# A re-ordered opening, a re-drawn plan and a gate on MLP stages in a fused attention and MLP kernel

## The chip, the cores and the metric

The kernel runs on one core of a Trainium2 chip. The metric is the device time of one execution in microseconds. A core has five engines that the text names as the profile does: PE (matrix products; PEld is its loading of weights), DVE (vector), ACT (scalar functions), POOL and SP (here only the issuer of DMAs). Each engine runs its instructions in the order in which they were put on it and waits on semaphores for the others. All arithmetic is in float32.

## The reference

x has 2048 tokens of width 512. There are 32 query heads of width 16 with one shared key head and one value head; the MLP has 1792 hidden features.

```python
xn = layernorm(x)                       # no scale, no bias, eps 1e-5
q = heads(xn @ wq); k = xn @ wk; v = xn @ wv
p = softmax(q @ k.T * 16 ** -0.5)
a = merge(p @ v) @ wo
h = xn @ w1 + b1
act = h * tanh(softplus(h))             # Mish
return x + a + act @ w2
```

## The kernel before

**Precision.** Products with weights are made of three matmuls in a fast float32 form: operand and weight are each split into a high part (a copy on ACT) and a low part (a subtraction on POOL), and hi x hi, hi x lo and lo x hi are summed (TERMS). The function split (L165) does it for a block of weights: one ACT and one POOL instruction of 128x512 each. A block goes through a buffer raw (three of them, L186), and its split form is stored to DRAM for later use (kept).

**Tiles.** Tokens are handled in four chunks c of 512 (CT), each four tiles of 128. xn is held transposed as X[c]. The queries of four heads (a unit u, 32 units in all) come out of half a block of 128 columns of wq: queries(c, mt) makes two units with 12 products, one for each of 4 parts of the width and 3 terms. hidden(c, f) (L597) makes one MLP tile of 128 features x 512 tokens, also with 12 products; there are 56. outputs(c, part, t) multiplies three (the last group two) of the finished tiles with w2, finals(c, t) the attention with wo.

**Softmax.** For each unit the scores are computed twice: once in the layout query x key, of which DVE takes the row maxima (maxima, L382; first_maxima, L388 for unit 0), and once in the layout key x query with the maximum subtracted inside the product (exps, L437), of which ACT takes the exponential. To subtract the maximum, negate_maxima and place_maxima (L393, L401) reduce the maxima of a unit, transpose them on PE (mt), split them on DVE (mhl) and send them by four DMAs to rows 48 to 49 and 112 to 113 of the unit's query tile QS (send, L410). values (L462) multiplies the exponentials pt with V and a column of ones, eight PE records per step of 128 keys.

**MLP stages.** A hidden tile h (buffer th, three of them) goes through these stages: ACT adds the bias (th); exponential: ACT, u = exp(h) (tu); square: DVE clamps u; product: POOL, n = u (u + 2); quotient: ACT, z = ln(n + 2) and r = exp(-z), then POOL five instructions with a result in h; act: ACT and POOL split h into the tile act. Each stage is put in a list (later, L139) with the step and the modelled time from which it may be put on its engines. run_due takes what is due, and flush(tags) puts stages on their engines at once when something needs them.

**The opening** (L861 to L979) loads x, normalises it, transposes it, projects keys and values and makes all queries. At the same time a loop over 32 pairs of score tiles (order, L936) finds the maxima of unit 0. In it first_maxima takes a pair of PSUM banks (tag e, two such pairs in the pool first_ps), and between the pairs PE is given either a part of transposes(2), transposes(3), keys_values(2), keys_values(3) (beside, L927) or products of the pieces of fill (fill_slot, L845). A piece is a set of 12 products that can be asked for one at a time. The pieces asked for first are those in urgent, the 15 left of the queries (L866); hidden tiles and the rest come after them. The opening ends when all queries are made; then six products of the first hidden tile are done and the second half of unit 0's maxima is placed.

**The planned part** (L984 to L1064) is written out as a string, PLAN, of 4270 letters. A letter is either one group of values (".") or one lane step: PE's array is used as two halves of 64 rows (lanes 0 and 1), and a lane step gives each half one matmul. A half may get a score tile for a maximum, a score tile for an exponential (single: a bank of its own, wide: one of a pair), half a product of a piece of fill (half), or nothing. A letter with the mark d drains PE first. The string comes from a planner that is not part of the kernel; the class Clock (L1067) follows it with prices for each step and tells when the stages in the list are due, by a time t of its own. POOL's modelled time (free) stands in Counted.

**Banks.** PSUM has eight banks. Before: the pool ps, which lives throughout, holds m (2 banks), misc (1) and o (1); first_ps has two pairs (4); late_ps, which takes their place, has e2 (2), e1 (1) and one more m (1). mbank (L128) takes a bank of kind m in turn.

Of the kernel before, what the change touches and what calls it, by code (L numbers as in the profile page):

```python
# [9 lines left out]
F32 = mybir.dt.float32  # L10
# [47 lines left out]
    "QQtisiisROQQcsiisRQckkkGyQQUQOQyG.oCssMisiysq.oqo.GQyQOEQ.qwo.sMoCsisMisysMs.mwe.qQOQSSQOOQOG.QSoq.sCCssMsii"  # L58
    "ysMs.mAo.GQyQ.QQUQSSQOUQ.GoCsiMsisCCq.ssCRQSOQOQOOQOQ..GyQQOOUQOQyOUQQ.qmCCiiMsisysM.oqo.Gsiy.qssiiysM.wAss."
    "sCCsVQQQSSUQ.yQQQU.ysMssiisCCq.my.Gwo.UQQOyQUOQO.qsCCsiMsisy.Gmy.QASQQOQUOQ.ssAw.GQSSQOQUOQyQUQ.qwo.sMssCCsM"  # L60
    "is.qym.GQy.USSQQQU.GCCssiMsisy.qoS.sMsysisM.mGy.ssyRQUOQOQSUo.ssMCsCisiG..GSSQQOQOUQy.sMCCssG.qSSQQOUQOQyq.m"
    "CsC.mGy.QUSSQQQU.wqCsiisMisysMs.mCo.qwSQOU.sCCssMsiisCCq.myq.QQUQSSQOUQOQ.MsCCssMs.qwo.GwSQ.AQSQQOUQOOoSG.wC"
    "ssM.mwS.QUQQOOQOAo.GsCCsisiisG.SSQUQQOOQy.qys.sMCCsssM.qSSQQOUQOQy.qosC.sMssCCsq.QSQUSQQOOG.GCCssiq.ACsss.Gy"
    "QQOOUQOQSSUQ.mCMCs.qCsCsMsis.QUQSSQQUOQ.Awm.UyQ.qmCCiisiMsisyMs..GSwQOOUQOQSSUQ.yqm.ysMssiisCCMss.AwQQ.QUQQO"
    "SSq.ossMC.qmy.MsyssM.qQQSSOQOQU.GCCssiMsisy.qSSQQ.GSSQQOG.tssMCCsis.USSQQQU.GCCssiMsisy.qwQS.GQQy.GSSQQOUQQS"
    "SG.oCqs.sMCssCsMis.qwSQ.wSQQUOQOyQUQ.qwo.sMssCCsiiMss.Gym.AQSQQOUQOOSQS..oMsCsisMisCsMw.UQQQOSSUQ.omC.MCsssC"
    "iiq.QQUSSQQOU.GCCssisMisy.qmy.GQSSQUQ.GwoiiiMssy.UQQwS.QQqy.GsCCsMs.qwSQOOQUOQ.SQGSQ.qwoiiiMsisCCMss..GSSQQO"
    "UQQSSG.SQGw.qsys.qsCCsiMsisCw.UQQSSQUQ.wQAQ.ooq.sCCsMssiisCCq.moUS.sMssCCq.mAo.QGSSQQU.CsMCssRUQSQS.sMssCCs."
    "GsCRUSQQ.QSUSm.ssMsCCsMsPSQUSQQOQ..AsCssiMsiiysMs.Awm.GQSSQOUQOQOSS..qCCssiMsisy.Gmy.GSSQQOUQQSSG.wSQG.mMy.s"
    "sqy.ssMsCCsMRQSSQUQ.mSQA.ysG.yQQQUOOQSSG.oCqs.sMssCCs.qow.sMCCsssM.oMoRQUOQOyQUQ.wwQ.QUQSSQQU.GsCCsiMsis.QUQ"  # L70
    "SSQQ.GyQQOOU.qCCssiMsisCCq.ms.AwQOQOUQOSSQUQ..qmCCiiMsisysiMs.SwUQQOOQSSQUQ..qwoiiiMsisCCsis.QQAw.QQUSSQQjsi"
    "MsiyssM..yQUQQOOQOOykq.oMCssisMisy.qssy.qym.sMssCCsPUQQ.ASQQQU.ysMssiisCCG.owG.QQUSSQQOU..qyssiiMsisCCq.Csqo"
# [20 lines left out]
    "QQ.ASQm.GCCssMs.sMsysis.UQSwQOUQOOQSS..ACsssiMisiCsMw.UQSSQQ.USQQQSE.ysMssiisCCMss..UQSSQQUQOOQSNssCs.sMsCCs"
    "s.ASQQQU.QQUSSQQG.GCCssiq.Aom.MCCsssM.qSSQQOUQOQyOUQ..qwoiiiMsisCCMss.qwo.GSSQQOUQOQy.qwo.sMsCsCsiiG..wSQQUO"
    "OQSQUSQ.GwoiiiMsisCCMss..qQSSQOUQOQew.mMsCCisMis.QQUSSQQOU.yqssiiisCCs.Gym.qCCssiMsisy.qww.UQQQSSUQO..qCCssi"
    "Msisyq.yQG.yQQQUOOQy.Uy.siiMiiCCMPOOSSUO.AS.Uy.MiiiyiMiii.PUSSOOOEOO.MCCiig.ACiiig.ASOOOOUOOOy.MiCCiM.Vy.UOy"
    "OOU.CCM.yiMiPSSU.yOU.y.MCCiiMPSSU.yOU.y.MiyiiiMPyOU.yOOO.."
# [4 lines left out]
def attention_and_mlp(ctx: ExitStack, tc: tile.TileContext, x, wq, wk, wv, wo, w1, b1, w2, out):  # L102
# [34 lines left out]
    now, queue = [-100], []  # L137
# [115 lines left out]
    def transposes(c):  # L253
        xt, FLAT[c] = x_tile(c, first if c > 1 else work)
        n = 2 if c < 2 else 1
        for d in range(0, DT, n):
            pt = first_ps.tile([P, 2, CT], F32, tag="e", name=f"xt{c}_{d}", bufs=2) if c < 2 else mbank(f"xt{c}_{d}")[:, None]
# [64 lines left out]
    def queries(c, mt):  # L322
# [5 lines left out]
        turn[1] += 1  # L328
        p = bank("o", f"q{c}_{mt}", 1) if beside == [] and turn[1] % 2 else misc(f"q{c}_{mt}")
# [58 lines left out]
    def first_maxima(kc, qt, pair):  # L388
        e = first_ps.tile([P, 2, CT], F32, tag="e", name=f"s0_{qt}_{kc}_{pair}", bufs=2)
        m = score_tiles(0, qt, kc, pair, {0: e[:, 0], 1: e[:, 1]})  # L390
        DVE.tensor_reduce(out=m, in_=e, axis=AX.X, op=ALU.max)
# [9 lines left out]
    def place_maxima(u, pairs=slice(0, 2)):  # L401
# [8 lines left out]
        def send():  # L410
            for a in range(2):
                for part in range(2):
                    SP.dma_start(
                        out=QS[u][a * 64 + 48 + part : a * 64 + 49 + part, pairs].bitcast(F32),
                        in_=m[a * n // 2 : (a + 1) * n // 2, part].bitcast(F32),
                    )
# [172 lines left out]
    read = {"u": 0.0, "z": 0.0}  # L589
# [7 lines left out]
    def hidden(c, f):  # L597
# [15 lines left out]
        def exponential():  # L613
            flush(("u", k - 1), ("n", k - 2))
# [15 lines left out]
        def product(u, n):  # L630
# [3 lines left out]
            later(2, lambda: quotient(n), ("n", k), max(POOL.free, read["z"]))  # L634

        def quotient(n):
            if late_pool:
# [10 lines left out]
            read["z"] = POOL.free  # L648
# [8 lines left out]
        later(max(1, 8 + k - 100 - now[0]), exponential, ("u", k), read["u"])  # L657
# [202 lines left out]
    with tc.tile_pool(name="first", bufs=1) as first, tc.tile_pool(name="first_ps", bufs=1, space=PSUM) as first_ps:  # L860
# [5 lines left out]
        urgent += [queries(*divmod(i, DT)) for i in range(1, NC * DT)]  # L866
# [31 lines left out]
        load_tokens(3)  # L898
        ask()
        flush(("wq", 0))  # L900
# [9 lines left out]
        flush(("wq", 1))  # L910
# [27 lines left out]
        skip = True  # L938
        for i, (kc, qt, pair) in enumerate(order):
# [289 lines left out]
```

## Time and profile before

| what | value |
|---|---|
| median of three runs | 1763.2 us (1760.71 to 1764.64) |
| profiled execution, its own time | 1763.43 us |
| its span, first to last instruction | 1761.7 us |
| mean granted PE clock | 0.97 |
| busy PE, DVE, ACT, POOL | 95%, 78%, 76%, 45% of the span |
| first lane matmul of the planned part | 121.87 us |
| first matmul of the first group of values | 140.4 us |

In the profile, a row of the timeline gives start and length in us, the engine, the line of the kernel, the operation, the tile written and the tile read, the shapes, and how many instructions were merged (x). What stands in brackets is the idle time of the engine ahead of the row and the instruction that ended it. A line of the waits names the waiting engine, tile and line, then the one waited for, the total in us, the number of waits and the longest. PE's clock is the share of full speed that was granted to it. Lines 1176, 1180, 1192 and 1200 are those of a helper that records every DVE, POOL or ACT operation, so there the tile's name tells what it is.

### The profile page before, as it was taken

How to read it: one execution, taken by the hardware profiler on the slowest of the kernel's cores; microseconds unless marked ns; L12 is line 12 of the kernel's file. 1: busy time of each engine (PE TensorE's matmuls, PEld its weight loads, DVE VectorE, ACT ScalarE, POOL GpSimd, SP SyncE). 2: the span in 40 equal slices, each digit the busy share in tenths (PEclk: the TensorE clock that was granted, in tenths of full speed). 3: DMA queues.
4: the chain of work that ended last, by engine and by line, in shares of the span. 5: the costliest groups of instructions: out<-in, count | busy, mean ns of one | idle time of the engine just before them, and what ended most of it. 6: DMA issues, size and time to landing. Idle time of an engine off the chain costs nothing.

```text
span 1761.7 us, 29992 instructions
## 1 busy us (share of the span) xinstructions
PE 1668.1 (95%) x11567; PEld 879.9 (50%) x11567; DVE 1369.5 (78%) x2269; ACT 1334.4 (76%) x1992; POOL 787.6 (45%) x699
## 2 busy tenths in 40 slices
PE   5989789799999999999999999999999999999998
PEld 4564444455455445554554555555455544545544
DVE  6638658688888878788888888888888888888821
ACT  3327568688788878788688888788688888877885
POOL 4534445455735444545136355445226264441532
PEclk8988889899999999999999999999999999999999
DMA  5555100304222212123122222122221222122030
GB/s 175 201 197 197 52 19 29 123 28 147 99 77 85 99 40 64 52 80 137 47 90 73 85 70 76 52 76 64 70 97 61 84 76 76 52 94 82 19 132 25
DMA packets 66821, 149.90 MB, mean 85 GB/s; under 512 B 9430, under 2 KB 19734, under 8 KB 66422
## 3 DMA queue, kind: packets, MB, share of 16 engines
q1 hardware_dynamic: 66678, 147.98, 24.8%
q8 instruction: 91, 1.49, 0.4%
q14 instruction: 52, 0.43, 0.1%
HBM read 97.98 MB, written 49.02 MB: 83 GB/s over the span
## 4 chain that ended last, share of the span: by engine, by line
PE 76%; POOL 5%; ACT 5%; DVE 4%; issue 2%; DMA 1%; POOLq 0%; ACTq 0%; DVEq 0%
PE o L466 25%; PE e L449 14%; PE s L373 13%; PE y L799 10%; PE h L799 10%; DVE nm L1192 3%; ACT pt L1200 3%; PE f L799 2%; POOL th L1176 2%; POOL tn L1176 1%; POOL tz L1176 1%; ACT tr L1200 1%; PE f_last L564 1%; ACT tz L1200 1%; DMA raw_w<-in_B_w_dram 1%
## 5 line engine op out<-in xcount | busy, mean ns | idle before, releaser
L1192 DVE TENSOR_REDUCE nm<-s 128x1 f32<-128x512 f32 (+1 forms) x2016 | 1281.4, 691 | 291.8 <-PE s L373 194.9
L1200 ACT ACTIVATE pt<-e 128x1024 f32<-128x1024 f32 (+1 forms) x1430 | 1047.9, 781 | 248.8 <-PE e L449 167.8
L373 PE MATMUL s<-KS,QS 48*128 48x512 f32 x2048 | 748.4, 437 | 2.6 <-DVE nm L1192 1.5
L449 PE MATMUL e<-QS,KS 64*128 64x512 f32 x2048 | 692.6, 434 | 37.9 <-ACT pt L1200 37.1
L466 PE MATMUL o<-pt,V 128*32 128x512 f32 x4096 | 544.9, 610 | 0.0
L373 PEld LDWEIGHTS s<-KS,QS 48*128 48x128 f32 x2048 | 356.5, 189 | 218.1 <-DVE nm L1192 172.9
L449 PEld LDWEIGHTS e<-QS,KS 64*128 64x128 f32 x2048 | 327.6, 188 | 255.1 <-ACT pt L1200 193.1
L799 PE MATMUL y<-w,act 64*128 64x512 f32 x1344 | 375.2, 407 | 8.2 <-ACT ty L1200 4.8
L799 PE MATMUL h<-X,w 64*128 64x512 f32 (+1 forms) x1338 | 370.7, 410 | 11.4 <-ACT th L1200 6.2
L799 PEld LDWEIGHTS y<-w,act 64*128 64x128 f32 x1344 | 241.3, 188 | 79.8 <-issue 33.9
L799 PEld LDWEIGHTS h<-X,w 64*128 64x128 f32 (+1 forms) x1338 | 246.6, 191 | 68.8 <-issue 19.0
L466 PEld LDWEIGHTS o<-pt,V 128*32 128x32 f32 x4096 | 84.8, 108 | 172.9 <-issue 167.7
L1180 POOL TENSOR_SCALAR tn<-tu 128x512 f32<-128x512 f32 x56 | 34.8, 621 | 295.8 <-DVE tu L1188 295.8
L1176 POOL TENSOR_TENSOR tn<-tn,tr 128x512 f32<-128x512 f32 x56 | 72.2, 1290 | 193.3 <-ACT tr L1200 193.2
L1176 POOL TENSOR_TENSOR y<-y,ty 128x512 f32<-128x512 f32 x80 | 103.2, 1290 | 120.7 <-ACT ty L1200 120.7
L1176 POOL TENSOR_TENSOR act<-th,act 128x512 fp32r<-128x512 f32 x56 | 72.5, 1295 | 65.0 <-ACT act L1200 65.0
L799 PE MATMUL f<-wo,ohl 64*128 64x512 f32 x288 | 75.9, 400 | 2.9 <-DVE yf L1176 2.5
L1176 POOL TENSOR_TENSOR tz<-tz,tn 128x512 f32<-128x512 f32 x56 | 72.3, 1291 | 4.7
L1176 POOL TENSOR_TENSOR th<-th,tn 128x512 f32<-128x512 f32 x56 | 74.3, 1326 | 0.0
L1176 POOL TENSOR_TENSOR th<-th,tz 128x512 f32<-128x512 f32 x56 | 72.2, 1289 | 4.4
L1176 POOL TENSOR_TENSOR tn<-tn,tu 128x512 f32<-128x512 f32 x56 | 71.9, 1284 | 4.7
L1176 POOL TENSOR_TENSOR ohl<-oc,ohl 128x512 fp32r<-128x512 f32 (+1 forms) x16 | 20.6, 1287 | 108.9 <-ACT ohl L1200 108.9
(86 smaller groups left out, 879.1 us busy)
## 6 DMA issues: line engine op xcount, KB each, us to landing
w<-w_dram SPq DMA_DIRECT2D x84, 512.0 KB
w_dram<-w SPq DMA_DIRECT2D x28, 512.0 KB
QS<-q_dram SPq DMA_DIRECT2D x62, 192.0 KB
q_dram<-q SPq DMA_DIRECT2D x16, 512.0 KB
wo<-wo_dram SPq DMA_DIRECT2D x16, 512.0 KB
o_dram<-ov SPq DMA_DIRECT2D x31, 256.0 KB
raw_w<-in_B_w_dram SPq DMA_DIRECT2D x28, 256.0 KB
xs<-in_A_x_dram SPq DMA_DIRECT2D x16, 256.0 KB
```

What stands on the lines that cost most here:

```text
L373: PE.matmul(tile, QS[u][rows, pair, qt * P : (qt + 1) * P], KS[rows, kc * CT : (kc + 1) * CT], start=True, stop=True,)
L449: PE.matmul(bank, KS[rows, kt * P : (kt + 1) * P], QS[u][rows, pair], start=True, stop=True)
L466: PE.matmul(O[u][h * 32 : (h + 1) * 32], V[:, kt], PT[(u * KT + kt) * HG + h], start=kt == 0, stop=kt == KT - 1,)
L564: PE.matmul(LAST[t], OHL[NC - 1, mt][:, i, t * P : (t + 1) * P], RINGED[NC - 1, "wo", mt][:, j], start=mt == 0 and k == 0, stop=mt == DT - ...
L799: PE.matmul(self.p, w[rows], x[rows], start=self.first, stop=last)
L1176: return self.engine.tensor_tensor(out=out, **kw)
L1180: return self.engine.tensor_scalar(out, *args, **kw)
L1192: return self.engine.tensor_reduce(out=out, in_=in_, **kw)
L1200: return self.engine.activation(out, in_, func, **kw)
```

## The change

- **Banks.** The banks m leave the pool that lives throughout. first_ps has three pairs of banks instead of two; late_ps gets all three m. In the opening mbank takes the first bank of such a pair, and all transposes take a pair too (one bank of it is used for chunks 2 and 3).
- **Order of fill.** urgent is filled later. The first two pieces asked for are hidden(0, 0) and hidden(0, 1). The blocks wq 1 to 3 are asked for behind them. The blocks w1 0 and w1 1 are split where wq 0 and wq 1 were, and wq 1 directly ahead of the loop.
- **The loop.** After each second pair of scores, six products are asked for, or two parts of beside with two products and one product behind them. Blocks are split in each pass. The order of beside is transposes(2), keys_values(2), transposes(3), keys_values(3). The opening goes on until all queries and the two hidden tiles are done (24 products of hidden tiles instead of 6).
- **Sends.** The four sends of unit 0's maxima, made for each of its two halves, are issued on ACT instead of SP.
- **Gate.** exponential and quotient ask, when they are run and not forced by a flush, whether the modelled time has reached the end of POOL's work on the tile before and whether that tile's stage is still in the list. If so they put themselves back in the list. The time that they had been given when they were listed falls away.
- **Plan.** PLAN has 4223 letters: 512 groups of values as before, 3711 lane steps (3758 before), of which 46 drain first (37 before). Halves of products: 2928 (2964 before); halves left empty: 462 (520 before). Clock.placed of unit 0 is 6.0 instead of 10.0.

```diff
 PLAN = (
...
-    turn, beside = [0, 0], [None]
+    turn, beside = [0], [None]
+
+    def pair_bank(name):
+        return first_ps.tile([P, 2, CT], F32, tag="e", name=name, bufs=3)
 
     def mbank(name):
-        turn[0] += 1
-        if late_ps and turn[0] % 3 == 0:
-            return late_ps.tile([P, CT], F32, tag="m", name=name, bufs=1)
-        return bank("m", name, 2)
+        return late_ps.tile([P, CT], F32, tag="m", name=name, bufs=3) if late_ps else pair_bank(name)[:, 0]
...
     def flush(*tags):
+        was, forced[0] = forced[0], True
...
+        forced[0] = was
+
+    def waits(tag, k, stage):
+        if forced[0] or not clock or clock.t >= read[tag] and (tag, k - 1) not in (e[2] for e in queue):
+            return False
+        later(0, stage, (tag, k), max(read[tag], clock.t + 0.5))
+        return True
...
-                    SP.dma_start(
+                    (SP if u else ACT).dma_start(
...
         def exponential():
+            if waits("u", k, exponential):
+                return
             flush(("u", k - 1), ("n", k - 2))
...
-            later(2, lambda: quotient(n), ("n", k), max(POOL.free, read["z"]))
+            later(2, lambda: quotient(n), ("n", k), POOL.free)
 
         def quotient(n):
+            if waits("n", k, lambda: quotient(n)):
+                return
...
-            read["z"] = POOL.free
+            read["n"] = POOL.free
...
-        later(max(1, 8 + k - 100 - now[0]), exponential, ("u", k), read["u"])
+        later(max(1, 8 + k - 100 - now[0]), exponential, ("u", k))
...
         first_queries = Piece(queries(0, 0))
-        urgent += [queries(*divmod(i, DT)) for i in range(1, NC * DT)]
...
         load_tokens(3)
+        for mt in range(1, DT):
+            WQ[mt] = block("wq", mt, f"wq{mt}", 1)
+        urgent += [queries(*divmod(i, DT)) for i in range(1, NC * DT)]
         ask()
-        flush(("wq", 0))
+        flush(("wq", 0), ("w1", 0))
...
-        flush(("wq", 1))
+        flush(("w1", 1))
...
-        beside[:] = [transposes(2), transposes(3), keys_values(2), keys_values(3)]
+        beside[:] = [transposes(2), keys_values(2), transposes(3), keys_values(3)]
 
         def beside_slot():
             while beside:
                 if next(beside[0], beside) is not beside:
-                    return 2
+                    return 3 if len(beside) % 2 else 2
                 beside.pop(0)
-            return 3
+            return 0
+
+        def fill_slots(n):
+            while n > 0 and done[0] < 12 * (NC * DT + 1):
+                n -= fill_slot(n)
...
+        flush(("wq", 1))
         for i, (kc, qt, pair) in enumerate(order):
...
             if i == 1:
-                fill_slot(12)
-            if i > 1:
-                n = beside_slot()
-                if n > 2:
-                    fill_slot(n)
-                else:
-                    if left[0] or skip:
-                        fill_slot(n)
-                    skip = not left[0] and not skip
-                flush(*(e[2] for e in queue if e[2][0] in ("w1", "wq")))
-                run_due(2)
+                fill_slots(12)
+            if i % 2 and i > 1:
+                n = 6
+                if beside:
+                    n = 5 - beside_slot()
+                    fill_slots(2)
+                    n = max(n - beside_slot(), 1)
+                fill_slots(n)
+            flush(*(e[2] for e in queue if e[2][0] in ("w1", "wq")))
+            run_due(2)
...
-        while done[0] < 12 * (NC * DT - 1):
-            fill_slot(12)
+        fill_slots(12 * NC * DT)
         flush(*(("q", *divmod(i, DT)) for i in range(NC * DT)), *(("u", i) for i in range(FT)))
         negate_maxima(0, slice(1, 2))
-        fill_slot(6)
         place_maxima(0, slice(1, 2))
...
-        self.placed = {0: 10.0}
+        self.placed = {0: 6.0}
```

More of the change, by code (lines that the diff above doesn't have):

```diff
@@ L63 @@
[L63 to L72, printed above, removed]
@@ L93 @@
[L93 to L97, printed above, removed]
+    "ssRtisRtssiRQAQSQUQQyQUtwCq.Gww.qow.soo.qsCCsMsRyQUQ.myq.ssCsCsVQOQQSSGQ.myq.ssMsCCsM.myq.wwUQ.QQUSSQQOUQtCq"
@@ new lines @@
+    "Cs.mMCCs.sMssCs.qsCRUQQSSQ.GwQSOUQ.GwQS.QQQUSSQOG.QSotsMisCCsMs.qmy.qoCs.GwCRQUQSSQUQ.myG.ssiysMs.yssq.ysssM"
+    "iisCCq.mwUS.QQUQOSQ.MsCssiMsiisCq.GQQSOOQUOQSQS.ssMsCCsiiG.ASQQQU.yUQQQ.GCCssisiiG.oAQQOOQOSQUo.Gmy.Mym.qQOQ"
+    "SSG.QSSQtMssCCsMs.yq.sssMCCsiiq.RUQSSQQOOG.MCCssq.qSSQQOG.qym.MssCCsMRQSSQUQ.Gym.qyss.qCCssiq.qCCssiG.GSQSQO"
+    "UQOQSQS..qCCssiMsiysMs.CAm.yQQQUOOQSSUQQ..sAsCsisMisy.mqy.QGSQSOQUOQ.GCCssiMsisy.wUw.QQUQyOQUQ.wGSQ.QUQyQOQU"
+    ".tssMCCsisq.QQQSUSQOQNsCsCsM.oqo.Gsys.Gym.UQSSQQUQOOQuSG.osMo.MsCCss.qCCss.GQQSSOQOOUQOQy.qmy.MssysiMs.qCCss"
@@ new lines @@
+    "iG.QQUSSQQOUQOQy.qwo.MsssCCMs.ossAis.ymG.yQUQQOOSQUo.GssCCisMis.UyQQQ.GSQSQOG.qCCssiMsisy.QUQSSQQU..qwStsiMs"
+    "isCCq..qCCssiMsisyq.wSGQ.QUSSQQQ.qsCCsiMsisysM.CAm.yQQQUOOQSSQUQ..oCssMisiCCsq.mAw.UQyQQOUQOOQSUw.qsCo.MssCC"
+    "sMs.mAo.GQyQ.QQQUSSQOUQtCsMw.GQQOOSQUSQ.tsCsC.qCCss.yQQQUOOQSSG.osqC.sMssCCs.qwQSOOQU.GCCssiM.qQSSQUQtCCMss."
+    ".UwSQQOUQOOyQUQ.mGy.qsys.ssMsCCsiMs.qSSQQOUQOQSSG.wQw.qoCisisM.MoCssiM.qSSQQOG.mAw.QQUQSSQjMssCCsM.ysMss.mQU"
+    "SSOQq.qCCss.MCmw.UQQSSQNssysiM.mq.USSQQQU.GCCssiMsisy.mqy.QGQy.QQQUSSQOOG.GsCCsisMis.USSQQQUOOQSSG.osC.GCCss"
@@ new lines @@
+    "iq.qoCsiMs.wGSQ.GSSQQOUQQSSG.osMo.sMCCsssM.qosC.mAo.GQyQOOUQQSSG.osMo.MsssCCM.myq.wSQG.QQUSSQQNsCCssMis.QUSQ"
+    "QSQ.QQNsCCsisMs.QUQSSQQUQ..qmCCiisiMsCw.qQSSQOQUOQyQOU..qCCssiMsisCCq.myqi.mAw.QUwSQOQUOQyQUQ.mAo.sMCCsssM.s"
+    "Mssy.QUQQSSG.QQUQSS.wsMCsiisMisysMk.mq.USSQQQU.GCCssiMsisy.qmy.QASm.MssCCsMs.oswVQOQSSQUQ.Gmy.qCCssiMsisy.RQ"
+    "USSQQUQ..qsCCsiMsisy.GwS.UQSSQQUQ.wCssMisiCCsq.yssq.woG.QUQyQOOUQQSQU.ssMsCisiMsis.RQQ.GyQQOOUQQSS.sMsysisMi"
+    "siysM.ymG.yQQUQOOQSSUQQ..GCCssiMsisy.qmyOOOq.GSSQQUQ.qCCssiMsisy.Gww.QUQQSSq.GwSQ.qoo.GouQGcy.mq.GymgcyG.ymG"
@@ new lines @@
+    ".ym.mAoMssiCsMs.ssCsVQOQSQUSQ.QQU.ssMCCssiMssCVSQQQ.USSQQQU.MCCsssM..MsyssMRSSQUQOQOQSS..MsyssiMsiiCCMm.mUSS"
+    "QOQU.QQSQS.sMsCCssMisisy.Gm.UwSQQOUQOSQUS.sMssCCsMis.CsAm.yQUQQOOQSSUQQ..GCCssiMsisyq.wQUSQ.QSQQS.sMsysisMis"
+    "y.GyQQ.QUQSSQQ.oMCssisMisiCsA.wUw.QUQQSSQUOQO.sMssCCsgis.Awm.qSSQQOOQUQ.GCCssiMsisy.qyQ.qym.GSQSQOQOOq.CsMCs"
+    "sRUQSQS.MssCCs.Aom.GSSQQUQ.GCCssiMsisCCq.oo.CAm.wQUQSOQOUQOOSGo.MssCCsMs.qoCsiiq.Gww.UQSSQQUQ.GQQSS.MssysiMs"
+    ".qsCCsiG.GSSQQOUQOQSSQ.mGy.MssysiM.qmy.GSSQQOU.ssMsCCRQUQSS.ssMsCCs.sCAm.AQSQQOUQ.qQQ.qCCssisMisy.qwSQOOUQOQ"
@@ L98 @@
+    ".qssCCiMsisiis.Ao.GQQSSOG.ysssMiisCCq.mwS.QQUSSQQU.ssMCCssiMsisy.Gw.UQSQQOUQOyQUQ..qCsCsiMsisy.wUQQSOQOUQ.Ms"
+    "sCCsiq.GSSQQOUQOQy.qmCC.qwo.qCCssiMsisyG.wQQUS.GQQSSOq.ysssM.MCCssq.AQoQOOUOOSS..CCssMiiiiyg.ASOOOOUOOOy.Mii"
+    "CCiMii..TSOOOOUOOy.MiiyiiiM.CCVOOOSSU.yOU.CCiVOOyOOU.AC.Miy.UOOyOOU.ACiiigiiy.My.MCCiig.ASOOOOU.y.MyiiiiMPyO"
+    "U.yU.yEOO.."
 )
@@ L124, in misc @@
         return bank("misc", name, 1)
-    turn, beside = [0, 0], [None]
+    turn, beside = [0], [None]
+    def pair_bank(name):
+        return first_ps.tile([P, 2, CT], F32, tag="e", name=name, bufs=3)
     def mbank(name):
-        turn[0] += 1
-        if late_ps and turn[0] % 3 == 0:
-            return late_ps.tile([P, CT], F32, tag="m", name=name, bufs=1)
-        return bank("m", name, 2)
-    now, queue = [-100], []
+        return late_ps.tile([P, CT], F32, tag="m", name=name, bufs=3) if late_ps else pair_bank(name)[:, 0]
+    now, queue, forced = [-100], [], [False]
+    read = {"u": 0.0, "n": 0.0}
     def later(delay, stage, tag, at=0.0, step=None):
@@ L256, in transposes @@
         for d in range(0, DT, n):
-            pt = first_ps.tile([P, 2, CT], F32, tag="e", name=f"xt{c}_{d}", bufs=2) if c < 2 else mbank(f"xt{c}_{d}")[:, None]
+            pt = pair_bank(f"xt{c}_{d}")[:, :n]
             for a in range(n):
@@ L327, in queries @@
         flush(("wq", mt))
-        turn[1] += 1
-        p = bank("o", f"q{c}_{mt}", 1) if beside == [] and turn[1] % 2 else misc(f"q{c}_{mt}")
+        turn[0] += 1
+        p = bank("o", f"q{c}_{mt}", 1) if beside == [] and turn[0] % 2 else misc(f"q{c}_{mt}")
         yield p, project(lambda i, d: wb[:, i, d], c, c == mt == 0)
@@ L388, in first_maxima @@
     def first_maxima(kc, qt, pair):
-        e = first_ps.tile([P, 2, CT], F32, tag="e", name=f"s0_{qt}_{kc}_{pair}", bufs=2)
+        e = pair_bank(f"s0_{qt}_{kc}_{pair}")
         m = score_tiles(0, qt, kc, pair, {0: e[:, 0], 1: e[:, 1]})
@@ L588, in attention_and_mlp @@
     A, used = {}, [0]
-    read = {"u": 0.0, "z": 0.0}
     def affine(out, x, scale, bias):
@@ L961, in attention_and_mlp @@
                     SP.dma_start(out=KS[r].bitcast(F32), in_=ones[:, None].to_broadcast([2, KT, P]))
-            if i in (20, 22, 24, 26):
-                flush(("v", (i - 20) // 2))
-            if i in (12, 18):
-                c = 2 + (i == 18)
+            if i in (24, 26, 28, 30):
+                flush(("v", (i - 24) // 2))
+            if i in (8, 14):
+                c = 2 + (i == 14)
                 flush(("lo", c))
```

41 lines of the change are left out of this document (15 added, 26 removed).

## The prediction

> **What bounds the kernel now.** I read the page first, for the shares; then a table by stage; then the order of work on each engine where a stage looked bad; then the waits.
>
> ```profile
> span 1761.7 us, 29992 instructions
> PE 1668.1 (95%) x11567; PEld 879.9 (50%) x11567; DVE 1369.5 (78%) x2269; ACT 1334.4 (76%) x1992; POOL 787.6 (45%) x699
> PEclk8988889899999999999999999999999999999999
> ```
>
> PE sets the end, and its clock is below full almost only in the first quarter. So a change there is worth most. The stage table (columns: stretch, length, busy time of PE, PEld, DVE, ACT, POOL, granted clock, DMA share, GB/s) splits that quarter:
>
> ```profile
> 35.00:60.00 25.00, 19.42 (x75) 11.61 (x75) 10.04 (x9) 10.41 (x20) 16.60 (x17) 0.72 0.31 109
> 60.00:92.00 32.00, 31.96 (x134) 17.76 (x132) 25.46 (x26) 8.40 (x15) 12.77 (x11) 1.00 0.57 222
> 121.90:140.40 18.50, 17.81 (x55) 10.95 (x54) 14.64 (x24) 4.51 (x8) 3.09 (x3) 0.50 0.41 137
> 140.40:206.40 66.00, 57.14 (x363) 29.26 (x362) 47.92 (x80) 46.12 (x70) 31.79 (x28) 0.89 0.40 140
> 206.40:273.20 66.80, 55.86 (x351) 28.36 (x353) 43.06 (x72) 44.35 (x66) 34.65 (x32) 0.87 0.07 23
> 273.20:333.30 60.10, 47.28 (x338) 22.91 (x340) 38.84 (x66) 41.68 (x65) 34.88 (x30) 0.91 0.22 77
> 1275.60:1321.10 45.50, 45.24 (x342) 24.42 (x341) 38.60 (x66) 36.76 (x55) 12.98 (x12) 1.00 0.28 94
> ```
>
> Three places lose time. **The opening** (to 121.9 us) has holes; here is PE there, with the idle time ahead of a row and its releaser in brackets:
>
> ```profile
> 27.70 0.74 PE L373 MATMUL s<-KS,QS 48*128 48x512 f32 x4
> 34.80 1.22 PE L799 MATMUL q<-X,wq 128*128 128x512 f32 x2 [6.36 <-ACT wq L1200]
> 39.62 4.64 PE L799 MATMUL q<-X,wq 128*128 128x512 f32 x10 [3.60 <-POOL wq L1176]
> ...
> 47.57 0.73 PE L799 MATMUL q<-X,wq 128*128 128x512 f32 x2 [1.80 <-ACT wq L1200]
> ...
> 83.63 0.50 PE L373 MATMUL s<-KS,QS 48*128 48x512 f32 x2
> 84.06 0.97 PE L799 MATMUL q<-X,wq 128*128 128x512 f32 x3
> ...
> 94.15 20.25 PE L799 MATMUL q<-X,wq 128*128 128x512 f32 x87
> 117.54 1.22 PE L799 MATMUL h<-X,w 128*128 128x512 f32 x2 [3.14 <-ACT w L1200]
> 119.65 2.08 PE L799 MATMUL h<-X,w 128*128 128x512 f32 x4 [0.88 <-POOL w L1176]
> 121.52 0.41 PE L405 MATMUL mt<-ident,nmr 128*8 128x128 f32 x1
> 121.87 0.79 PE L799 MATMUL h<-X,w 64*128 64x512 f32 x1
> ```
>
> The scores start at 27.7; then PE waits 6.36 + 3.60 + 1.80 = 11.8 us for a wq block to be split, and 3.14 + 0.88 at the seam to the planned part, for w1. **The start of the planned part**: the first product with V comes 18.5 us after the first lane step, at half clock throughout. **The burst of MLP tiles after it**: the three stretches from 140.4 to 333.3 hold 48 groups of values (eight matmuls each) and, counted in the plan's letters, 129 + 117 + 108 = 354 lane steps. The last stretch of the table, at full clock, holds 16 groups and 113 steps in 45.5 us, and one group takes 0.99:
>
> ```profile
> 1277.55 0.99 PE o L466 x8
> ```
>
> So a step costs (45.5 - 16 x 0.99) / 113 = 0.26 us, and 48 groups with 354 steps should take 47.5 + 92 = 140 us. They took 192.9: 53 us too long. ACT's waits between 120 and 300 us say why in part:
>
> ```profile
> ACT tu L1200 <- POOL tn L1176: 8.2, 2, 4.9
> ACT th L1200 <- POOL act L1176: 7.9, 4, 3.8
> ACT pt L1200 <- issue: 6.8, 1, 6.8
> ...
> ACT act L1200 <- POOL th L1176: 3.4, 1, 3.4
> ACT tz L1200 <- POOL th L1176: 2.6, 1, 2.6
> ```
>
> ACT runs in order. A stage of the MLP (tu, act, tz) that is put on it before POOL is done holds up the exponentials (pt) behind it, and PE waits for those.
>
> **The change, part by part.**
>
> *Opening, w1 first.* The first two pieces of fill become MLP tiles h0 and h1. Their blocks are split early (before transposes(0) and ahead of the last half of q0), so the 12 products at the second pair of scores no longer wait for a wq block: the 6.36 goes. wq1 is split just ahead of the loop. On POOL it falls behind normalise(2) and two KS rows, and ahead of normalise(3), which now holds wq2 and wq3:
>
> ```profile
> 27.93 3.03 POOL L1180 TENSOR_SCALAR xs<-xs,v,y 128x512 f32<-128x512 f32 x4 [3.21 <-issue]
> 31.04 2.57 POOL L1176 TENSOR_TENSOR KS<-kvs,KS 16x512 fp32r<-16x512 f32 x2
> 35.16 3.02 POOL L1180 TENSOR_SCALAR xs<-xs,v,y 128x512 f32<-128x512 f32 x4 [1.54 <-issue]
> 38.14 1.43 POOL L1176 TENSOR_TENSOR wq<-raw_wq,wq 128x256 fp32r<-128x256 f32 x2
> ```
>
> So wq1 is whole at 33.6 + 1.4 = 35.0. What is late next is DVE: statistics(3) and root(3) hold the second maximum.
>
> ```profile
> 34.90 1.22 DVE L1192 TENSOR_REDUCE nm<-s 128x2 f32<-128x1024 f32 x1
> ```
>
> With three pairs of banks PE can do four pairs of scores and h1's 12 products (to about 32 us); then the first transpose wants the bank of the second pair, free at 36.1. I start the loop's steady part at 36, after one new wait of about 4 us in place of 11.8.
>
> *Two pairs, six products.* From the rows at 83.63 and 84.06: a pair takes 0.43 and three products with the change of mode 0.90 (steps of 1.33; two make 2.66). Back to back a product takes 20.25 / 87 = 0.233, so the change costs 0.2, and half of the changes go: 0.43 + 0.23 + 6 x 0.233 + 0.2 = 2.26. But DVE needs 2 x 1.22 = 2.44 for two maxima, so DVE becomes the bound there: 2.55 a step. Steps with keys and values: 0.66 + 9 products x 0.233 + 0.2 = 2.96. Steps with transposes now draw their bank from the same three as the scores (four draws a step, each transposed bank held by two ACT copies): between 2.5 (DVE) and 3.6; I take 3.1, nearer the middle because nothing shows it. 4 x 3.1 + 4 x 2.96 + 7 x 2.55 = 42 us, so the loop ends at 78.
>
> *Tail.* done must reach 204 (180 for 15 q, 24 for h0 and h1), of which 90 are through. 114 left, by 0.233: 26.5 us. The q stores may hold it:
>
> ```profile
> 98.00 1.26 ACT L1200 ACTIVATE q<-q 128x512 f32<-128x512 f32 x2 [1.53 <-PE q L799]
> ...
> 115.71 1.26 ACT L1200 ACTIVATE q<-q 128x512 f32<-128x512 f32 x2 [0.95 <-DMA q_dram<-q]
> ```
>
> Six q in 17.7 us is 2.95 each, against 12 x 0.233 = 2.8: 28 us. The first lane step then comes at 106.5, not 121.87: **-15.4** (bounds: -5, if transposes take 3.6 and the stores pace all of the loop; -21, without the new wait).
>
> *The seam and the sends.* The 18 more products are h0 and h1 whole, but the plan's first half step is now of h2, whose w1 block nothing splits ahead of time: the 3.14 us wait moves behind the seam. In front of that split ACT now issues the four sends of the maxima:
>
> ```profile
> 122.28 2.50 SPq L413 DMA_DIRECT2D QS<-mhl  x4
> ```
>
> They cost SP 2.50 us; ACT, for which no row shows it, 0 to that again. I take +3.5 for split and sends together. What is queued behind them is that split, and PE behind it. Before, SP had reached the sends when their data came, so nothing is gained by leaving its queue. The Trainium skill speaks against this edit too (Trainium Kernel Development and Optimization, Key Constraints: another issuing engine only saves the sequencer's issue time); by it as by the row the move is worth nothing or less.
>
> *Start of the plan.* 27 steps stand before the first values, not 33, and the first exponential at the 14th, not the 24th. At full clock that is 27 x 0.26 + 3.5 = 10.5 us; at half clock (twice 0.233 a step) 16. I take 14 for 18.5, because the wait ahead of it is as long as the one that left the clock at 0.50: **-4.5**. The Trainium skill (TensorE: Matmul & The Clock Gate, Part 1) would have full clock back after one busy window of about 3.4 us; the row 121.90:140.40, with PE busy 17.81 of 18.50 us at 0.50, differs. By the page the start would come out near 12 us, 2 better; the sum goes by the row.
>
> *The plan.* 3711 lane steps for 3758, six of the 47 counted above: 41 x 0.26 = 10.7 less. Drains 46 for 37, of which three more are above: six at 0 to 0.6 us, say 0.3: 1.8 more. **-8.9**. 18 of the 47 steps are the products moved to the opening, 29 were half-empty.
>
> *The gate, and two tiles ahead.* An exponential or quotient is put back when POOL by the program's count is not done, so the 8.2 + 2.6 us above go. More is in the buffer of h (th, three of them): h3 can't leave its bank until act(h0) is through, which waits for the late pool. Before, the first act came at 182 us:
>
> ```profile
> 182.42 1.27 POOL L1176 TENSOR_TENSOR act<-th,act 128x512 fp32r<-128x512 f32 x1 [5.64 <-ACT act L1200]
> 183.72 0.69 ACT L1200 ACTIVATE th<-h,b1s 128x512 f32<-128x512 f32 x1 [1.38 <-POOL act L1176]
> ```
>
> Now h0 and h1 run through exp, log and POOL's five products in the opening, beside PE's tail (POOL 16.6 of 25 us there at the fullest), and only act is left. Of the seven tiles that the burst begins with, five are left, and two of them find a free buffer. I take a third of the 53 us, **-16**; bounds 0 (the chain of a tile is as long as before and the tiles come as fast) and -45.
>
> **Sum**: -15.4 - 4.5 - 8.9 - 16 = -44.8. The profiled run took 1763.43 us, 1.7 outside its span, and the median is 1763.2, so they are one: 1763.4 - 44.8 = **1719**. Own range 1704 to 1734.
>
> **Rivals.**
> (1) *The burst stays.* PE is held by POOL's chain of each tile, whatever the order on ACT; POOL's 32 to 35 us per stretch don't shrink but for two tiles. For it: th waits for act, which no gate touches. Against it: two tiles are ahead. 1763.4 - 28.8 = 1735.
> (2) *The opening doesn't shrink as far.* Bank turns and q stores pace it and it ends at 117: -5 in place of -15.4, 1729; with (1), 1745.
> (3) *The burst dissolves*, PE stays warm from the seam on: -45 in place of -16 and -8 at the start: 1686.
> (4) *Slower.* A gated stage goes to the back of the queue and is then forced, with all its chain, when an output or the tile three later needs it; forced stages don't ask the gate, and ACT then sits through POOL's rest. A worst case of such a stop is in the trace (another cause, same effect on PE):
>
> ```profile
> PE e L449 <- ACT pt L1200: 10.6, 1, 10.6
> ```
>
> At about half of that, 5 us each, it takes nine forced tiles of the 54 to eat the 45 us; with 14 the time is 1789. Against it: the gate delays by half a microsecond at least and POOL is 45% busy.
> (5) *The gate does nothing by itself*, since ACT's waits for POOL are few; it is inside (1).
>
> **Chances.** Forecast 0.50, (1) 0.22, (2) 0.12, (3) 0.09, (4) 0.07. About 0.2% (3.5 us) is what a measurement of this kernel can tell from no change; a sliver of (1) with (2) lands there. Faster 0.89, same 0.04, slower 0.07. The range takes in (1) and (2) together and part of (3): 1695 to 1750.
>
> **What would show it.** Opening: no wait on wq above 2 us, first lane matmul (64 rows) between 102 and 112 us, loop steps of 2.5 us with DVE without gaps; wrong, if the tail's q copies wait for stores by more than 1 us each or transposes for maxima. Seam: one PE wait of 3 to 4 us on ACT w behind L405. Start: first o 12 to 15 us after it. Burst: stretches of 16 groups near 55 us, and the waits of ACT tu and tz for POOL near zero. If the late stretches at full clock take more than 46 us each, the plan is worse than its count of steps and the forecast falls; so it does if ACT's waits for POOL th or tn grow.

## The result and the profile after

The changed kernel takes **1688.5 us** (median, 1687.64 to 1689.59); the kernel before, in the same comparison, 1762.0. The ratio is 0.9582 with a 95% interval of 0.9565 to 0.9598. The forecast was 1719 with a range down to 1695: the sign was right, the size was 30 us short. The time is within 3 us of rival (3), in which the burst dissolves, but it came about by other parts than (3) names.

The head of the page after:

```profile
span 1686.8 us, 29994 instructions
PE 1631.5 (97%) x11549; PEld 862.1 (51%) x11549; DVE 1367.7 (81%) x2269; ACT 1334.0 (79%) x1997; POOL 784.7 (47%) x695
PEclk9989999999999999999999999999999999999999
```

DVE, ACT and POOL are busy for as long as before (1369.5, 1334.4 and 787.6 us then); PE has 37 us less, and its clock is below full in fewer slices. The stage table (stretch, length, busy time of PE, PEld, DVE, ACT, POOL, granted clock, DMA share, GB/s), with the start of the plan, the three stretches of 16 groups of values that stood for the burst, and a late stretch:

```profile
113.30:132.40 19.10, 14.00 (x52) 7.42 (x52) 11.95 (x19) 7.80 (x13) 8.16 (x7) 0.73 0.51 179
132.40:186.60 54.20, 50.02 (x339) 22.61 (x339) 44.08 (x74) 40.43 (x61) 21.33 (x19) 0.94 0.45 154
186.60:236.40 49.80, 49.30 (x365) 25.94 (x363) 44.93 (x76) 42.59 (x64) 30.66 (x27) 1.00 0.08 28
236.40:286.30 49.90, 47.91 (x346) 24.25 (x344) 42.01 (x70) 43.58 (x69) 34.18 (x29) 1.00 0.36 121
...
1251.20:1299.50 48.30, 48.12 (x367) 26.09 (x367) 41.83 (x70) 40.30 (x61) 25.06 (x22) 1.00 0.24 77
```

The 48 groups took 192.9 us before and take 153.9 now, with POOL's load in them smaller (86 us for 101). The opening shows both halves of its story on PE:

```profile
32.01 0.73 PE L383 MATMUL s<-KS,QS 48*128 48x512 f32 x4
37.29 1.09 PE L270 MATMUL xt<-ident,xs 128*128 128x128 f32 x4 [4.56 <-DVE nm L1209]
...
81.01 5.64 PE L812 MATMUL q<-X,wq 128*128 128x512 f32 x23
87.99 5.78 PE L812 MATMUL q<-X,wq 128*128 128x512 f32 x24 [1.34 <-ACT q L1217]
95.33 17.11 PE L812 MATMUL q<-X,wq 128*128 128x512 f32 x72 [1.55 <-ACT q L1217]
112.28 0.27 PE L415 MATMUL mt<-ident,nmr 128*8 128x128 f32 x1
113.28 0.47 PE L383 MATMUL s<-KS,QS 48*128 48x512 f32 x1 [0.73 <-PE mt L415]
117.66 0.79 PE L812 MATMUL h<-X,w 64*128 64x512 f32 x1 [3.92 <-ACT w L1217]
```

The waits on wq are gone and the one for the second maximum stands in their place (4.56 us, foreseen as "about 4"). The tail of 119 products takes 31.3 us, and the wait on the split of w1 stands behind the seam, as foreseen (3.92).

**Where the 74.9 us of span went.** For each stretch I take the time less 0.26 us per lane step and 0.99 per group of values, and call the rest its excess. The row of the 41 steps is thus their count at that price and not a measurement of its own; drains, and the 19 us behind the last group of values, are in the excess. The position in the plan is read from the matmuls with V, whose 1st and 49th groups start at 140.4 and 333.3 us before, at 132.4 and 286.3 after.

| part | foreseen | measured |
|---|---|---|
| opening, to the first lane matmul (121.87 to 113.28) | -15.4 | -8.6 |
| from there to the first values (18.5 to 19.1) | -4.5 | +0.6 |
| 41 lane steps fewer behind that (3725 to 3684), drains | -8.9 | -10.7 (41 x 0.26) |
| excess of the first 48 groups (53.2 to 17.5) | -16 | -35.7 |
| excess of the rest (92.6 to 72.1) | 0 | -20.5 |
| sum | -44.8 | -74.9 |

So the opening gave little more than half of what it was to give, and the stalls in the planned part gave three and a half times as much (56.2 us for 16).

### The profile page after: what moved, and what is told of

Read it like the earlier page. It is cut to its first block, busy times and chain, and to the rows that moved or that the text cites. A ratio compares the mean times of both kernels' runs of the same rounds, so it can differ in the third digit from the quotient of the medians.

```text
span 1686.8 us, 29994 instructions
## 1 busy us (share of the span) xinstructions
PE 1631.5 (97%) x11549; PEld 862.1 (51%) x11549; DVE 1367.7 (81%) x2269; ACT 1334.0 (79%) x1997; POOL 784.7 (47%) x695
## 4 chain that ended last, share of the span: by engine, by line
PE 86%; DVE 5%; ACT 3%; DMA 3%; issue 2%; POOL 2%; SPq 0%; ACTq 0%; POOLq 0%; DVEq 0%
PE o L476 29%; PE e L459 17%; PE s L383 14%; PE y L812 11%; PE h L812 11%; DVE nm L1209 3%; PE f L812 3%; DMA q_dram<-q 1%; ACT pt L1217 1%; DMA raw_w<-in_B_w_dram 1%; PE f_last L574 1%; ACT q L1217 1%; PE kv L307 1%; POOL q L1193 1%; PE mt L415 0%
## 5 line engine op out<-in xcount | busy, mean ns | idle before, releaser
L383 PE MATMUL s<-KS,QS 48*128 48x512 f32 x2048 | 735.3, 432 | 5.3 <-DVE nm L1209 2.7
L459 PE MATMUL e<-QS,KS 64*128 64x512 f32 x2048 | 690.5, 429 | 12.5 <-ACT pt L1217 11.2
L383 PEld LDWEIGHTS s<-KS,QS 48*128 48x128 f32 x2048 | 346.0, 186 | 210.4 <-DVE nm L1209 174.6
L812 PE MATMUL y<-w,act 64*128 64x512 f32 x1344 | 366.9, 401 | 1.5
L812 PE MATMUL h<-X,w 64*128 64x512 f32 (+1 forms) x1320 | 358.7, 403 | 5.2 <-ACT w L1217 3.9
L812 PEld LDWEIGHTS h<-X,w 64*128 64x128 f32 (+1 forms) x1320 | 237.4, 186 | 55.0 <-issue 21.1
```

Source lines behind the costliest of these rows:

```text
L383: PE.matmul(tile, QS[u][rows, pair, qt * P : (qt + 1) * P], KS[rows, kc * CT : (kc + 1) * CT], start=True, stop=True,)
L459: PE.matmul(bank, KS[rows, kt * P : (kt + 1) * P], QS[u][rows, pair], start=True, stop=True)
L812: PE.matmul(self.p, w[rows], x[rows], start=self.first, stop=last)
```

## Experiments: gate, plan and opening apart

All times are medians; the kernel before ran beside each set, at 1761 to 1763 us.

**1. The gate alone taken out, and alone put in.** In the first kernel the change stands but for the gate; in the second only the gate is added to the kernel before.

```diff
         def exponential():
-            if waits("u", k, exponential):
-                return
...
         def quotient(n):
-            if waits("n", k, lambda: quotient(n)):
-                return
...
-            later(2, lambda: quotient(n), ("n", k), POOL.free)
+            later(2, lambda: quotient(n), ("n", k), max(POOL.free, read["n"]))
...
-        later(max(1, 8 + k - 100 - now[0]), exponential, ("u", k))
+        later(max(1, 8 + k - 100 - now[0]), exponential, ("u", k), read["u"])
```

> The changed kernel without the gate (stages get their times as in the kernel before). Theory G: the gate is what removed the waits of ACT for POOL, in the burst (36 us gained beyond its steps) and in the later stretches (20 us gained beyond theirs): 1725 to 1745 us, and the waits ACT tu <- POOL tn and ACT tz <- POOL th come back with 20 to 30 us. Theory T: the two tiles that are ahead and the new plan did it, and the gate is worth at most the few us by which ACT waited for POOL: 1688 to 1698.

> The kernel before with the gate alone; opening and plan as before. Theory G: 1710 to 1730 us (the burst and the later bumps go, the opening and the steps stay). Theory T: 1750 to 1762, the th buffers still wait for the first act at 182 us, so the stretch from the first to the 49th group of values stays above 180 us (192.9 before).

Measured: without the gate 1715.6 us (ratio to before 0.9738, 0.9724 to 0.9753); with the gate alone 1734.2 (0.9844, 0.9829 to 0.9858). So the gate is worth 27.1 us in the one kernel and 27.6 in the other. Both theories missed the time: Theory T allowed the gate at most 9.5 us in the one kernel and 12 in the other, Theory G asked it for 32 us and more. One sign of each came: with the gate alone the stretch from the first to the 49th group stays above 180 us (183.0), as T has it, and without the gate ACT's wait of tu for tn is back with 18.5 us, as G has it; that of tz for th is not. The excess says where the gate works: with the gate alone it falls by 10 us in the first 48 groups (53.2 to 43.5) and by 17 later (92.6 to 75.4); the gate taken out of the changed kernel costs 5 in the first 48 (17.5 to 22.1) and 21 later (72.1 to 93.6). What PE waits for exponentials in the whole run, in the kernel before and with the gate alone:

```profile
PE e L449 <- ACT pt L1200: 37.1, 23, 10.6
PE e L458 <- ACT pt L1212: 10.7, 15, 3.2
```

That is 26.4 us of the 27.6. In the changed kernel it is 11.2 us, without the gate 24.8, half of the 27.1. The waits of ACT in one late stretch, first without the gate:

```profile
ACT tu L1213 <- POOL tn L1189: 7.1, 2, 5.1
ACT pt L1213 <- PE s L383: 2.1, 3, 1.5
ACT pt L1213 <- PE e L459: 1.8, 6, 0.6
```

and in the same 16 groups of the changed kernel:

```profile
ACT pt L1217 <- PE e L459: 2.3, 7, 0.6
ACT pt L1217 <- PE s L383: 1.8, 4, 0.8
ACT act L1217 <- POOL th L1193: 0.6, 1, 0.6
```

The stretch took 54.3 us and 46.0. The letters are the same 16 groups' in both. Two stages tu put on ACT too early hold it for 7.1 us, and the whole stretch is 8.3 us longer. Over all the run the page of before had shown this wait and its twin:

```profile
ACT tu L1200 <- POOL tn L1176: 20.2, 8, 4.9
...
ACT tz L1200 <- POOL th L1176: 8.6, 3, 4.5
```

Their sum, 28.8 us, is near the gate's price of 27.6. It isn't an exact price: in the kernel without the gate 18.5 us of wait stand against 27.1. In the changed kernel neither wait is in the list.

**2. The old plan in the changed kernel.** The letters of before, with the first 18 halves of each lane left empty, because the opening has done their products:

```diff
+    skipped = [0, 0]
+
     def one_half(a):
+        if skipped[a] < 18:
+            skipped[a] += 1
+            return
         done[0] += 0.5
```

> The changed kernel (opening, banks, gate) with the letters of the plan of before; the first 18 halves of each lane in it, whose products the opening has done, are left empty. The plan's 47 steps come back, 0.26 us each: 12 us, so 1700 us if only their number counts (Theory T without the plan, and Theory G both say so, 1697 to 1705). If the order of the letters is what keeps PE from waiting, 1710 to 1730, with the stretches of 16 groups after the 48th showing the bumps of before (56 and 54 us).

Measured: 1714.1 us (0.9731, 0.9714 to 0.9747). So the new letters are worth 25.6 us with this opening and the gate, and the new opening 20.1 under the old letters (1734.2 to 1714.1). Number against order: 41 steps behind the first values are 10.7 us at 0.26 each; the excess of the first 48 groups is 36.5 with the old letters and 17.5 with the new; that of the rest is nearly the same (74.2 and 72.1), and the first values come 5.5 us earlier with the old (126.9 to 132.4), whose empty halves don't wait for a block. Most of the bumps that I expected in the late stretches were not there: the 16 groups from the 129th took 55.9 us before and 48.1 here, though those from the 337th still took 54.1. With the gate in, the letters make their difference in the burst.

**3. The new plan with the old opening,** the gate in, and the 18 products left of h0 and h1 at the opening's end:

```diff
-        fill_slot(6)
+        while done[0] < 12 * (NC * DT + 1):
+            fill_slot(12)
```

> The kernel before with the gate and the new plan: its own opening (two pairs of banks, wq first), at the end of which the 18 products left of h0 and h1 are done, whose MLP stages then all run in the planned part. The opening is 4.2 us longer for the 18 products and about 3 for the split of the second w1 block. If the new opening is worth only the time at which it ends (8 us to the first values) and the early MLP stages nothing: 1700 to 1707. If the two tiles whose stages are through before the plan starts carry the burst: 1715 to 1730, with PE waiting on th in the first 100 us of the plan.

Measured: 1746.6 us (0.9912, 0.9898 to 0.9927), 12 us *slower* than the old plan with the gate and the old opening without the 18 products, and above both expectations. The first lane matmul comes at 131.9, the first values 6 us later than in that kernel (146.2 to 140.2), and the first 48 groups have an excess of 62.8 us for 43.5. PE's waits between 120 and 350 us:

```profile
PE h L811 <- ACT th L1213: 23.1, 3, 9.1
...
PE y L811 <- ACT th L1213: 8.8, 1, 8.8
```

**4. The early stages by themselves.** The changed kernel, but exponential to quotient of h0 and h1 start in the planned part:

```diff
-        later(max(1, 8 + k - 100 - now[0]), exponential, ("u", k))
+        later(1 if k < 2 else max(1, 8 + k - 100 - now[0]), exponential, ("u", k), step=0 if k < 2 else None)
...
-        flush(*(("q", ...)), *(("u", i) for i in range(FT)))
+        flush(*(("q", ...)))
```

> The changed kernel, but the MLP stages of h0 and h1 (exponential to quotient) start only in the planned part instead of beside the opening's tail; products, letters, banks and gate stay. If it is these early stages that carry the burst with the new plan: 20 to 45 us slower than the changed kernel (1708 to 1733), with PE waiting for th between the first and the 49th group of values, as in the run with the old opening and the new plan. If the burst's gain comes from the order of the letters alone: 1686 to 1693.

Measured: 1730.1 us (0.9826, 0.9812 to 0.9841), **41.6 us** slower, within the first expectation; the excess of the first 48 groups is 64.1. PE in that stretch, three of its stops:

```profile
183.61 0.79 PE L812 MATMUL h<-X,w 64*128 64x512 f32 x1 [8.57 <-ACT th L1217]
...
207.03 0.79 PE L812 MATMUL h<-X,w 64*128 64x512 f32 x1 [9.06 <-ACT th L1217]
...
232.61 1.66 PE L812 MATMUL y<-w,act 64*128 64x512 f32 x2 [8.85 <-ACT th L1217]
```

and POOL's last stage of three tiles in the same kernel (h1, h2 and h3):

```profile
181.58 1.26 POOL L1193 TENSOR_TENSOR act<-th,act 128x512 fp32r<-128x512 f32 x1 [0.74 <-ACT act L1217]
...
205.00 1.26 POOL L1193 TENSOR_TENSOR act<-th,act 128x512 fp32r<-128x512 f32 x1 [0.74 <-ACT act L1217]
...
230.58 1.26 POOL L1193 TENSOR_TENSOR act<-th,act 128x512 fp32r<-128x512 f32 x1 [0.74 <-ACT act L1217]
```

Each stop ends 2 us behind the start of an act: the new tile waits for one of the three th buffers, ACT and PE wait with it, and tiles pass at the pace of the chain, 23 to 26 us each. Tile h2, for one, holds its buffer from 132.5 us (th) to 206.3 (the end of its act), 73.8 us, a third of which is 24.6. In the changed kernel act of h0 and h1 is through at 130 us and no wait of PE for th is in the list. So the new plan needs the two tiles' stages ahead of it: moving them alone costs 41.6 us. They ran beside the loop's last steps, where POOL had time (66.1 to 83.1 us), and not beside the tail.

They also have a price in the opening, which this run shows. Without them the tail is one row without a gap, though q has two buffers as in the changed kernel:

```profile
79.34 27.69 PE L812 MATMUL q<-X,wq 128*128 128x512 f32 x119
```

The first lane matmul then comes at 107.87 us and not at 113.28. So 46.6 us more in the burst (64.1 for 17.5) stand against 5.4 less in the opening.

## Experiments: the opening

**5. Sends on SP again.**

```diff
-                    (SP if u else ACT).dma_start(
+                    SP.dma_start(
```

> The changed kernel with unit 0's sends on SP again. As the prediction has it (nothing gained by leaving SP's queue, up to 2.5 us of ACT ahead of the split at the seam): 1685 to 1689 us, the wait on ACT w at the seam 2.6 us shorter. Rival: on SP the sends stand behind the last q store and a wait for POOL (SP issued that store at 116.39 us, 2 us after ACT's first send), so they land 3 to 5 us later, the first exponential waits for them, and the time is 1690 to 1694.

Measured: 1686.7 us (0.9578, 0.9563 to 0.9592) against 1688.5: the interval takes in the changed kernel's ratio, so no difference is shown. The wait at the seam is 1.79 us for 3.92: the sends did stand ahead of the split.

**6. The split ahead of the sends.**

```diff
         flush(*(("q", ...)), *(("u", i) for i in range(FT)))
+        flush(("w1", 2))
```

> The changed kernel with h2's block of w1 put on ACT and POOL directly after the last q, ahead of unit 0's last four sends. PE's wait of 3.92 us at the seam on ACT w becomes about 1.5; by the prediction's price for it, and if the clock stays at full speed for it, 1683 to 1687 us; if the first exponentials wait for the sends instead, which are now 0.6 us later, 1688 to 1690.

Measured: 1685.0 us (0.9568, 0.9552 to 0.9584); the wait at the seam is

```profile
114.91 0.61 PE L812 MATMUL h<-X,w 64*128 64x512 f32 x1 [0.84 <-ACT w L1218]
```

and the first values come at 129.0 instead of 132.4. The wait is 3.1 us shorter and the whole 3.5, though the interval still meets that of the changed kernel.

**7. Four buffers for q.**

```diff
-        q = first.tile([P, 2, CT], F32R, tag="q", name=f"q{c}_{mt}", bufs=2)
+        q = first.tile([P, 2, CT], F32R, tag="q", name=f"q{c}_{mt}", bufs=4)
...
```

To make room, the small buffers fu go from 3 to 2, fz and fr from 2 to 1.

> The changed kernel with four buffers for q instead of two (three small buffers of the MLP stages in the opening are cut for the room: fu 3 to 2, fz and fr 2 to 1). If the tail is paced by the two buffers (ACT's copy of a q waits 2.3 + 0.8 us for stores of the q two before): PE's gaps of 1.3 and 1.6 go, 114 products take 26.6 us and the first lane step comes at 108 to 110 us instead of 113.3; 1683 to 1686 us. If it is paced by what the DMA engines move (307 GB/s between 104 and 112 us): 113 again, 1687 to 1690.

Measured: 1681.9 us (0.9562, 0.9536 to 0.9588; the four executions lie between 1680.4 and 1690.4), the first lane matmul at 108.5. The interval meets that of the changed kernel; number 9, with these buffers and the split ahead, is clear of it. The tail is

```profile
80.10 27.60 PE L812 MATMUL q<-X,wq 128*128 128x512 f32 x119
107.54 0.27 PE L415 MATMUL mt<-ident,nmr 128*8 128x128 f32 x1
```

that is 0.232 us per product without a gap, where the changed kernel took 31.3 us. What a buffer is held for in the changed kernel can be read from its chain of waits:

```profile
102.36 0.61 ACT q L1217
...
102.99 0.64 ACT q L1217
...
103.76 1.31 POOL q L1193
...
105.08 2.88 DMA q_dram<-q
```

From 102.36 to the next copy into the same buffer at 108.07 it is 5.71 us; two buffers turn every 2.86 us, and PE makes a q in 12 x 0.232 = 2.79. So two buffers leave no slack, but they alone don't make the gaps: at 2.86 for 12 products the tail would take 28.4 us, and number 4 has two buffers and 27.69. What makes them are the stages of h0 and h1, which stand ahead of a q's low part on POOL:

```profile
81.85 1.29 POOL L1193 TENSOR_TENSOR th<-th,fz 128x512 f32<-128x512 f32 x1
83.09 2.53 POOL L1193 TENSOR_TENSOR q<-q 128x512 fp32r<-128x512 f32 x2
...
87.34 1.26 ACT L1217 ACTIVATE q<-q 128x512 f32<-128x512 f32 x2 [5.34 <-DMA q_dram<-q]
```

The q that ACT copied at 73.04 us has its low part at 83.09 here; in number 4 the same q is copied at 71.36 and has it at 72.75. Its store and the next copy into the buffer follow as late, and PE's first gap stands at 87.99. Two edits remove the gaps, then: more buffers, or no MLP stages in the way. The DMA engines were not the limit: with four buffers they moved 308 GB/s between 92 and 104 us, where the changed kernel moved 230.

**8. DVE's statistics in parts.** bn_stats of chunk 3 behind the 4th to 7th pair, one token tile each, root and normalise behind the last:

```diff
-            if i == 0:
-                statistics(3)
+            if 2 < i < 7:
+                statistics(3, i - 3)
+            if i == 6:
                 root(3)
                 normalise(3, POOL)
```

> The changed kernel with statistics(3) taken one token tile at a time at the 4th to 7th pair of scores instead of whole behind the first, and root(3) and normalise(3) behind the 7th. If PE's 4.56 us wait for the second maximum is what DVE's statistics cost: the wait goes, the first lane step comes 3 to 4.5 us earlier, 1684 to 1686 us. If the tail is paced by the q stores, which start no earlier for it: 1687 to 1690, PE's gaps in the tail grow by as much.

Measured: 1685.8 us (0.9560, 0.9546 to 0.9575). The 4.56 us wait is gone (the first transpose starts at 32.61), and the first lane matmul comes at 111.1, only 2.2 earlier: the tail's gaps on the q copies are about as long as they were (1.31 and 1.86 for 1.34 and 1.55). The time is that of the first expectation and the first lane matmul falls short of it; the interval meets that of the changed kernel.

**9 and 10. Together:** four buffers with the split ahead of the sends, and these with the statistics in parts.

> The changed kernel with four q buffers and h2's block of w1 split ahead of unit 0's last sends. The two edits alone gave -6.6 and -3.5 us against the changed kernel; they are at different places (tail and seam), so -10: 1677 to 1680. If the seam's wait is then for the last q copy or the sends instead: 1680 to 1682.

> The changed kernel with all three: four q buffers, h2's block ahead of the sends, statistics(3) in parts. With four buffers the stores no longer pace the tail, so the 3 to 4.5 us of the statistics should count in full: 1673 to 1677 us. If they are lost in the tail all the same: 1677 to 1680.

Measured: 1679.3 us (0.9524, 0.9509 to 0.9539) and **1676.8** (0.9510, 0.9495 to 0.9524). The first is the sum of its two parts, within the noise. The statistics add 2.5 us, not 3 to 4.5, though the time is within the first expectation; the intervals of the two kernels meet. They were worth 2.7 alone, so they don't grow when the tail has no gaps. The last kernel is faster than the kernel before and the changed kernel, clear of both intervals, and 10.6 of its 12 us over the changed kernel lie in the opening and at the seam: its first values come at 121.8 us, and from there on it is like the changed kernel (1552.5 us to its end; 1554.4 there).

```profile
span 1674.3 us, 29987 instructions
PE 1628.8 (97%) x11549; PEld 860.9 (51%) x11549; DVE 1365.9 (82%) x2269; ACT 1334.2 (80%) x1997; POOL 784.7 (47%) x695
```

## Why the prediction was right in sign and wrong in size

**The step that failed** is the term of -16 us for the gate and the two tiles ahead, together with the stretches behind 333 us, which have no term in the sum. Measured are -35.7 us in the first 48 groups and -20.5 behind them. The opening failed too, the other way (-8.6 for -15.4). That the time came out near rival (3), 1686, is luck: (3) has -45 for the burst, 8 us less at the start and the whole -15.4 of the opening, where -35.7, +0.6 and -8.6 were measured, and it has nothing for the 20.5 us behind the burst.

- **The gate: the wrong row.** "So the 8.2 + 2.6 us above go" priced it, inside the 16, by the waits between 120 and 300 us. The same list for the whole run has 20.2 + 8.6, and the gate measures 27.1 and 27.6. The prediction gave the stretches behind 333 us nothing; number 1 puts 17 and 21 us of the gate there. Rival (5), that the gate does nothing by itself, falls. So does (4): ACT's waits of tu and tz for POOL, where a forced stop would show, are out of the list.
- **Two tiles ahead: the mechanism was right, the size was not.** Of the seven tiles "two of them find a free buffer" has about 5 of the 16 us left beside the gate; number 4 puts the early stages alone at 41.6 us under the new plan. The row to price it with was there: POOL's first act at 182 us, and the next ones 17 to 26 us apart. I had the wait ordered by buffers but not the chain's length as the pace of the tiles, which is what two finished tiles break. Under the old plan the new opening lowers the burst's excess by only 7 us (43.5 to 36.5), so much of the worth comes with letters that use them.
- **Opening, the new wait and the steps: mostly right.** The 11.8 us of waits for wq went, the wait for the second maximum came (4.56), the steps with transposes took 3.0 to 3.3 us (3.1 foreseen) and those with keys and values 2.95 (2.96). Of the last steps, those with a transpose of V between their pairs of scores ran longer than the 2.55 put for them, 2.8 to 3.4 us between 69.69 and 78.76. The loop ended at 81 us and not at 78.
- **Opening, the tail: too small a term.** I had the q stores and took 2.95 us for each 12 products from rows in which PE was not held, 28 us (the 106.5 has half a microsecond more than 78 + 28); 119 products took 31.3. I put the stages of h0 and h1 beside the tail at no price. They hold POOL ahead of it, and two buffers for q can't make that good; numbers 4 and 7 show it. Of the rival (2), "Bank turns and q stores pace it", this part came true in part. The sign "the tail's q copies wait for stores by more than 1 us each" came, but it says little by itself: such waits of 2.3 to 2.6 us stand in number 4 too, and PE has no gap there.
- **Seam: right in place and price** (3.92 for 3.5), and moving the sends shows no difference. The start of the plan was foreseen too short: 14 us for 19.1, since the clock stayed at half until about 128 us and PE stood idle for 5.1 us there, 3.92 of them for the split.
- **The plan: right in number** (41 steps, 10.7 us at 0.26 each), with one thing missed: 19 us that the new letters save in the burst. The sign against it, late stretches above 46 us, came with 48.3 us, but it was badly put: that row holds 123 steps, the one of before 113, and 16 x 0.99 + 123 x 0.26 is 47.8.

**Open.** Why the old letters keep 36.5 us of excess in the burst isn't settled: that run also begins with 36 empty halves, so its first tile h2 starts later, and the order of the letters and this lateness weren't taken apart. What the early stages are worth under the old letters wasn't run.

## What to carry to other kernels

Price an engine's in-order waits from the list of the whole run, not from the stretch in which they were noticed: waits of ACT, which is not the bound, held up the exponentials that PE needs, and 28.8 us of them came back here as 27.6. Where a chain of stages turns over few buffers, the time for which a tile holds its buffer, divided by the buffers, is the pace (73.8 / 3 = 24.6 us in number 4); a few items finished ahead, in a stage with idle engines, can be worth more than all the steps that they save. They aren't free there: ask what else those engines must do in that stage, and whether its buffers have slack for the delay.

## What was not expected of the hardware

The half clock at the seam lasted a different time for a like gap of PE: from 117 to 141 us before (gaps of 3.14 and 0.88), and to about 128 after (3.92). The row 113.30:132.40 has a mean of 0.73 for it, the one of before 0.50. The prediction put the half clock down to this wait, and two runs speak against that: in number 6, where PE's longest wait there is 0.84 us, the clock is at half from 115 to 125 us, and in number 2, where the longest is 0.73, from 116 to 136. At the start of the plan the three kernels with the old letters have 20 to 24 us at half clock and the ten with the new ones 7 to 14; what in the letters decides it wasn't tested. The Trainium skill (TensorE: Matmul & The Clock Gate, Part 1) puts the return to full clock at one busy window of about 3.4 us; the traces of before and after differ, with 24 and 10 us.
